# Turning q' two tiles at a time, and new places for the pieces of Wr

## The chip, the cores and the metric

The kernel runs on one core of a Trainium2 chip. The metric is the time of one execution on the device in microseconds; lower is better. Everything is 32-bit floating point outside; inside, each operand of a matmul is split into a high and a low part, so that three matmuls (high x high, high x low, low x high) stand for one exact product.

## The reference

`x` is 2048 x 576. Two branches are mixed by a gate for each row:

```python
g = sigmoid((x * gate_w).sum(-1, keepdims=True))
# A: linear attention, 32 heads of 18, phi(t) = where(t > 0, t + 1, exp(t)) + 1e-6
q, k, v = split(x @ wqkv); pq, pk = phi(q), phi(k)
kv  = einsum("bhsd,bhse->bhde", pk, v);  z = sum of pk over s
num = einsum("bhqd,bhde->bhqe", pq, kv); den = einsum("bhqd,bhd->bhq", pq, z) + 1e-6
a = (num / den).reshape(S, D) @ wo
# B: real part of a two-dimensional Fourier transform, with given matrices
y = dft_seq_re @ (x @ dft_hid_re.T) - dft_seq_im @ (x @ dft_hid_im.T)
return g * a + (1 - g) * y
```

## The kernel before, in words

TensorE works on tiles of 128 rows of `x` (16 tiles, `NT`) and half rows of 288 columns. The stages follow each other on TensorE:

- **k'** (`k_half`): k' = phi(x Wk) tile by tile. The first four tiles go together (L520), the other twelve one by one in the loop over `i`. Each tile is 2 halves of 14 matmuls. ScalarE and VectorE make phi (`feature`: two ScalarE operations and one VectorE operation for a half), split k' (`k_split`) and split the coming x tiles (`split_next`).
- **k'^T x** (L676): 20 steps; in step `step` four chunks of x are multiplied with the k' tiles. The chunks come by `xg_load` from SP's queue, are split by `xg_next` (tile `c`, raw `craw`), and stand in a ring of four. `kv_step` follows with Wv. In the same loop the sum over k' (`zacc`), Wq's load and split, and Wo's loads are placed.
- **q'** (`q_tile`): q' = phi(x Wq), 16 tiles of 28 matmuls; one more column pair of Wq gives the gate's logit, which ScalarE turns to exp(-logit), and VectorE to 1 + that and its reciprocal. kv and Wo are joined to one 576 x 576 matrix M (`build_kv`, `build_m`, `move_m`, `split_m`). `normalise` is a generator of four steps for a pair of tiles and divides q' by its denominators.
- **M stage**: `transposed(i)` turns tile i of q' with TensorE (four blocks of 128 columns, and a fifth for the 64 columns that are left, written twice side by side in `twice`), splits it to `qs`, and 2 x 14 matmuls with M follow; ScalarE scales with the gate, and POOL's queue stores `att`.
- **Hidden** (L945) and **sequence** (L1100), twice: the Fourier branch by Strassen-like products of seven: first x with Wr (`Hidden.run`), then with the matrix `cr`, then Wi and `ci`. `Matrix.load` brings the pieces of `cr` and `ci` (`craw` there), `make` adds and splits them; `row` tiles hold the branch so far.

For the last stages operands are prepared beside the earlier ones, in generators that are advanced by `go` at places written out by hand. `Left(k, ...)` loads a piece of x on POOL's queue, adds, splits and stores it (`xb`, `xm`): five steps. `right(w, ...)` gives three pieces of Wr or Wi (`wb`, stored to `wm`), of six steps: load, two additions, two additions, high, low and store, low and store (the third piece, 96 rows, has a low of 32 rows and one store). Each `next` puts its instructions at that point of the engines' order.

The order of ScalarE and VectorE is the order of the program from the k' stage on, that of SP's queue throughout, and that of TensorE from the first `Hidden.run` on; TensorE is ordered by a planner before that. POOL has its queue to itself and takes its DMAs in order. `begin_after` ties a POOL load to an earlier ScalarE instruction (`done[-1]`). PSUM has eight banks of which each `bank()` takes one. SBUF is one arena in which `at` places tiles by hand, so a piece can only be where the bytes are free: a load into bytes that a store still reads waits for it.

Of the kernel before, what the change touches and what calls it, by code (L numbers as in the profile page):

```python
# [8 lines left out]
F = mybir.dt.float32  # L9
R = mybir.dt.float32r  # L10
# [4 lines left out]
P = 128  # L15
# [116 lines left out]
def kernel(  # L132
# [108 lines left out]

    acc = [at(ACC_AT + i * D * 4, [P, D], F, "acc") for i in range(NT)]

# [337 lines left out]
    def xg_next(lo_of=lo_of):  # L581
        if xg_raw:
# [84 lines left out]
    for c in range(5):  # L667
        ps = [bank(), bank()]
        passes = FULL if c < KC else FULL[:2]
        for q in range(NCU):  # L670
# [21 lines left out]
            if step == 0:  # L692
                add(zacc, acc[0], acc[1])
            elif step < NT - 1:
                add(zacc, zacc, acc[step + 1])
            if step == NT + 1:
# [12 lines left out]
            for k, j, o in ((6, 2, SLOT_AT + 15104), (NP, 6, ACC_AT)):  # L709
# [15 lines left out]
    def q_tile(i):  # L725
        xs = split.pop(0)
        if i == 0:
            split_next()
        for h in range(2):
            ps = bank()[:, :QH[h]]  # L730
            run(ps, steps(xs, lambda j: wqt.row(h, j)))
            g = gate[:, i:i + 1]
# [3 lines left out]
        nc.vector.tensor_scalar(g, g, 1.0, None, op0=ALU.add)  # L736
        nc.vector.reciprocal(out=g, in_=g)
        load_next()
        if i:
            split_next()  # L740

    pz_ring = Ring(T_AT + 40960, D * 4, 4)

    def normalise(k):
# [10 lines left out]
        for i in range(2):  # L755
            a = acc[2 * k + i].rearrange("p (h d) -> p h d", d=DH)
            nc.vector.scalar_tensor_tensor(a, a, EPS,
                                           d[:, i].unsqueeze(2).to_broadcast([P, H, DH]),
                                           op0=ALU.add, op1=ALU.mult)
            twices.append(at(T_AT + 36864 + (2 * k + i) % 8 * 512, [P, 2, REST], F, "twice"))  # L760
            rest = acc[2 * k + i][:, KC * P:]
            nc.vector.tensor_copy(out=twices[-1],
                                  in_=rest.unsqueeze(1).to_broadcast([P, 2, REST]))
            yield

    twices = []
    norms = (part for k in range(NT // 2) for part in normalise(k))


    qs_ring = Ring(T_AT + 50176, XS, 2)  # L770

    def transposed(i):

        xs, _ = new_xs("qs", qs_ring)
        banks = [bank(), bank()]
        twice = twices.pop(0)
        for c in range(5):
            a = acc[i][:, c * P:(c + 1) * P] if c < KC else twice.rearrange("p a b -> p (a b)")
            nc.tensor.transpose(banks[c // KC][:, (c % KC) * P:(c % KC + 1) * P], a, ident)  # L779
        hi_of(xs[:, 0:4], banks[0])  # L780
        lo_of(xs[:, 5:9], banks[0], xs[:, 0:4])
        hi_of(xs[:, 4], banks[1][:, :P])
        lo_of(xs[:, 9], banks[1][:, :P], xs[:, 4])
        return xs

# [5 lines left out]
    mraw = at(T_AT + 23040, [P, KC, D], F, "mraw")  # L791
    mrest = at(T_AT + 32256, [P, D], F, "mraw")

    def build_kv():
# [40 lines left out]
    def split_m(h):  # L835
        hi_of(mhi[:, :KC, half(h)], mraw[:, :, half(h)])
        lo_of(mlo[:, :, half(h)], mraw[:, :, half(h)], mhi[:, :KC, half(h)])
        hi_of(mhi[:, KC, half(h)], mrest[:, half(h)])
        lo_of(mhi[64:, KC, half(h)], mrest[64:, half(h)], mhi[64:, KC, half(h)])

    def m_row(h, j):
        return mhi[:, j, half(h)] if j <= KC else mlo[:, j - 5, half(h)]

    store_rest()
    wr_forms, wr_pieces = right(wr, wr_rest, ((0, T_AT + 60416), (1, T_AT + 76544),
                                              (2, T_AT + 60416)))
    xs_ring.at[3] = T_AT + 105664
    load_next()
# [6 lines left out]
    q_tile(2)  # L855
    next(norms)
    q_tile(3)
    go(wr_pieces[0])
    next(norms)
    build_m((0, 1))  # L860
    for i in range(4, NT):
        q_tile(i)
        build_m({4: (2, 3), 5: (4,)}.get(i, ()))
        for g in range(2 * (i - 4), min(2 * (i - 3), NG)):
            move_m(g)
        for k, j, n in ((0, 4, 2), (0, 5, 1), (0, 6, 2), (1, 4, 1), (1, 7, 2), (1, 8, 1),
                        (1, 11, 2), (2, 9, 1), (2, 13, 2), (2, 14, 1)):
            if i == j:
                go(wr_pieces[k], n)
        if i in (5, 8, 11, 12, 13):  # L870
            go(norms)
        if i == NT - 3:
            nxt = transposed(0)
        if i in (9, 10):
            split_m(i - 9)

# [182 lines left out]
    def sequence(m, g, src, dst, last=None, between=None):  # L1059
        late, held, stores, rest_lows = [], [], [], []  # L1060
        for n in range(NP * NB):
            j, b = divmod(n, NB)
            if b == 0:
                ps = {k: bank()[:, :HALF] for k in PRODUCTS}
# [3 lines left out]
            c = m.ready.pop(0)  # L1068
            m.load(n + 3)
            while stores:  # L1070
                stores.pop(0)()
            if n == 2:
                tick()
            if m.raws:
                new = m.make()
# [7 lines left out]
            if n == 1:  # L1083
# [3 lines left out]
                del pending[-2:]  # L1087
            elif n == 2:
                while rest_lows:
                    rest_lows.pop()()  # L1090
            end = last is not None and j == NP - 1
# [60 lines left out]
    made = {}  # L1152
    plan = {
        2: [(0, 1)], 3: [(0, 1)], 4: [(0, 1)], 5: [(0, 1)], 6: [(0, 1)], 7: [(1, 1)], 8: [(1, 1)],
        9: [(1, 1)], 10: [(1, 1)], 11: [(1, 1)], 12: [(7, 1)], 13: [(7, 1)], 14: [(7, 1)],
        15: [(7, 2)],
    }
    for i in range(NT):
        qs = nxt
        if i + 1 < NT:  # L1160
            nxt = transposed(i + 1)
        for h in range(2):
            ps = bank()
            run(ps[:, :HALF], steps(qs, lambda j: m_row(h, j)))
            done.append(nc.scalar.activation(acc[i][:, half(h)], ps[:, :HALF], AF.Copy,  # L1165
                                             scale=gate[:, i:i + 1]))
        nc.gpsimd.dma_start(out=att[i], in_=acc[i])
# [5 lines left out]
        for k, j, o in ((0, 0, SLOT_AT), (1, 3, SLOT_AT + 7 * XF),  # L1173
                        (NP - 1, 8, T_AT + (NP - 2) * TPAIR)):
            if i == j:
                left = Left(k, o, done[-1])
                made[k] = left.make()
                if k < 2:
                    hidden.take_x(k, left.c)
        if i == 7:  # L1180
# [4 lines left out]
        for p, j in ((1, 8), (2, 11), (3, 15)):  # L1185
            if i == j:
                hidden.load_rest(p)
        if i == 11:
            hidden.load_pair(2)
        if i in (13, 15):  # L1190
            for k in (0, 2) if i == 13 else (4, 6):
                hidden.load_x(3, k)
    nc.vector.tensor_scalar(gate_n, gate, -1.0, 1.0, op0=ALU.mult, op1=ALU.add)
# [35 lines left out]

    paced.enter_context(tc.manual_schedule(engines={mybir.EngineType.PE}))  # L1230
    first.load_rest(4)
# [96 lines left out]
```

## Time and profile before

| | us |
|---|---|
| three runs | 726.32, 727.18, 729.66; median 727.18 |
| the profiled execution | 726.95, of which 725.2 are the span of its instructions |
| TensorE busy | 720.0 (5444 matmuls) |
| VectorE, ScalarE, POOL busy | 600.5, 335.7, 57.1 |

The span is the time from the first to the last instruction of the profiled execution. A busy time is the union of an engine's instructions. "PE" is TensorE's matmuls and "PEld" its weight loads, which overlap them; "DVE" is VectorE, "ACT" ScalarE, "POOL" GpSimd, "SP" the engine that only issues DMAs. In a group's row stand the line of the helper that recorded it, the engine, the operation, out<-in by the names of the program, the shape, the count, then the busy time, the mean of one in ns, and the idle time of the engine before them with what ended it. L173 is the high of every split (`hi_of`), L183 the low (`lo_of`), L193 an addition (`add`), L203 a matmul of `run`.

### The profile page before, as it was taken

What the parts mean: (1) busy time and instruction counts of PE and PEld (TensorE: products, weight loads), DVE (VectorE), ACT (ScalarE), POOL (GpSimd) and SP (SyncE); (2) the same over time, 40 slices, a digit from 0 to 9 for tenths busy, and PEclk for the clock granted to TensorE, in tenths of its full rate; (3) what the DMA queues carried; (4) which work ended last, traced back from release to release, by engine and by line L of the source; (5) the groups of instructions that cost most, each with busy time, mean ns of one, the idle gap of its engine ahead of it and who ended that gap; (6) DMA issues with size and microseconds to landing.
All of it is one profiled execution on the core that took longest, in us unless ns stands there. A gap on an engine that the chain in (4) does not pass through costs nothing.

```text
span 725.2 us, 13882 instructions
## 1 busy us (share of the span) xinstructions
PE 720.0 (99%) x5444; PEld 718.8 (99%) x5444; DVE 600.5 (83%) x995; ACT 335.7 (46%) x522; POOL 57.1 (8%) x98
## 2 busy tenths in 40 slices
PE   9999999999999999999999999999999999999998
PEld 9999999999999999999999999999999999999997
DVE  5789867589999948989999989767889988788884
ACT  5998346588644444453344334323535332232231
POOL 1011300051032110000000000000000000000000
PEclk9999999999999999999999999999999999999999
DMA  7376795676477999744475675889963543444440
GB/s 256 90 275 221 265 341 176 239 219 231 149 238 285 338 324 379 236 154 139 163 246 176 226 242 179 295 294 396 380 228 129 174 146 136 159 147 150 153 153 33
DMA packets 54372, 158.82 MB, mean 219 GB/s; under 512 B 6436, under 2 KB 11108, under 8 KB 53284
## 3 DMA queue, kind: packets, MB, share of 16 engines
q1 hardware_dynamic: 45060, 118.90, 47.9%
q0 software_dynamic: 8960, 38.65, 14.6%
q8 instruction: 43, 0.70, 0.4%
q10 hardware_dynamic: 288, 0.39, 0.1%
q14 instruction: 21, 0.17, 0.1%
HBM read 115.05 MB, written 41.39 MB: 216 GB/s over the span
## 4 chain that ended last, share of the span: by engine, by line
PE 93%; DMA 3%; DVE 2%; issue 1%; POOL 0%; ACT 0%; SPq 0%; DVEq 0%; ACTq 0%; POOLq 0%
PE bank L1100 48%; PE bank L203 23%; PE bank L945 14%; PE bank L676 3%; PE bank L520 2%; PE bank L779 1%; DMA craw<-in_xg_dram 1%; DMA wraw<-in_wv_dram 1%; DMA xm<-xb 1%; DVE ys L193 1%; PE bank L229 1%; POOL xb L389 0%; PE bank L658 0%; DVE c L183 0%; ACT xb L173 0%
## 5 line engine op out<-in xcount | busy, mean ns | idle before, releaser
L1100 PE MATMUL bank<-fh,c 128*128 128x288 f32 x1792 | 355.1, 294 | 0.3 <-DVE c L183 0.3
L1100 PEld LDWEIGHTS bank<-fh,c 128*128 128x128 f32 x1792 | 286.8, 188 | 0.5 <-DVE c L183 0.5
L1100 PE MATMUL bank<-fl,c 128*128 128x288 f32 x896 | 263.6, 294 | 0.0
L173 ACT ACTIVATE c<-craw 128x1792 fp32r<-128x1792 f32 (+1 forms) x84 | 121.5, 1449 | 187.5 <-DVE craw L193 169.2
L1100 PEld LDWEIGHTS bank<-fl,c 128*128 128x128 f32 x896 | 168.7, 188 | 0.0
L183 DVE TENSOR_TENSOR c<-craw,c 128x1792 fp32r<-128x1792 f32 (+4 forms) x86 | 142.0, 1654 | 6.2 <-ACT c L173 6.1
L193 DVE TENSOR_TENSOR craw<-craw 128x256 f32<-128x256 f32 (+1 forms) x192 | 98.3, 512 | 23.9 <-DMA craw<-in_ci_dram 11.7
L203 PE MATMUL bank<-wd,xs 128*128 128x288 f32 (+1 forms) x784 | 105.9, 296 | 0.0
L203 PEld LDWEIGHTS bank<-wd,xs 128*128 128x128 f32 x784 | 104.6, 188 | 0.1
L945 PE MATMUL bank<-wf,xf 128*128 128x288 f32 x588 | 91.1, 295 | 0.0
L945 PEld LDWEIGHTS bank<-wf,xf 128*128 128x128 f32 x588 | 83.5, 189 | 0.0
L203 PE MATMUL bank<-mw,qs 128*128 128x288 f32 x448 | 63.2, 297 | 0.0
L676 PE MATMUL bank<-pk,c 128*128 128x288 f32 x448 | 61.2, 296 | 0.1
L676 PEld LDWEIGHTS bank<-pk,c 128*128 128x128 f32 x448 | 59.9, 189 | 0.5 <-ACT c L173 0.4
L203 PEld LDWEIGHTS bank<-mw,qs 128*128 128x128 f32 x448 | 59.9, 188 | 0.2 <-DVE qs L183 0.2
L367 DVE SCALAR_TENSOR_TENSOR acc<-bank,e 128x288 f32<-128x288 f32 x64 | 28.1, 453 | 19.8 <-ACT e L366 19.1
L193 DVE TENSOR_TENSOR ys<-bank,ys 128x288 f32<-128x288 f32 x63 | 28.8, 457 | 15.1 <-PE bank L1100 12.0
L183 DVE TENSOR_TENSOR fl<-fl,fh 128x864 fp32r<-128x864 f32 (+1 forms) x32 | 34.6, 1093 | 6.6 <-ACT fh L173 5.3
L173 ACT ACTIVATE fh<-fl 128x864 fp32r<-128x864 f32 (+1 forms) x32 | 29.9, 951 | 16.6 <-DVE fl L193 15.0
L945 PE MATMUL bank<-wf,xr 96*128 96x288 f32 x112 | 33.3, 298 | 0.0
L1165 ACT ACTIVATE acc<-bank,gate 128x288 f32<-128x288 f32 x32 | 16.1, 502 | 35.0 <-PE bank L203 34.8
L193 DVE TENSOR_TENSOR ys<-ys,bank 128x288 f32<-128x288 f32 x47 | 21.2, 450 | 12.3 <-PE bank L1100 11.8
(107 smaller groups left out, 664.9 us busy)
## 6 DMA issues: line engine op xcount, KB each, us to landing
xf<-xm SPq DMA_DIRECT2D x42, 512.0 KB, 9.0
craw<-in_cr_dram SPq DMA_DIRECT2D x32, 512.0 KB, 3.9
craw<-in_ci_dram SPq DMA_DIRECT2D x32, 512.0 KB, 3.4
xraw<-in_xa_dram SPq DMA_DIRECT2D x28, 320.0 KB, 3.5
xm<-xb POOLq DMA_DIRECT2D x8, 1024.0 KB, 6.8
wf<-wm SPq DMA_DIRECT2D x14, 576.0 KB, 5.8
xr<-xr SPq DMA_DIRECT2D x14, 448.0 KB, 8.0
xm<-xb POOLq DMA_DIRECT2D x8, 768.0 KB, 6.4
```

The source lines that it names most:

```text
L173: return nc.scalar.activation(dst, src, AF.Copy, bias=bias)
L183: nc.vector.tensor_tensor(out=dst, in0=src, in1=hi, op=ALU.subtract)
L193: nc.vector.tensor_tensor(out=dst, in0=a, in1=b, op=op)
L203: nc.tensor.matmul(ps, a, b, start=(n == 0), stop=(n == len(pairs) - 1))
L229: nc.tensor.matmul(warm[:, :P], ones_f, ones_f, start=True, stop=True)
L367: nc.vector.scalar_tensor_tensor(dst, ps, 0.0, e, op0=ALU.max, op1=ALU.add)
L520: nc.tensor.matmul(ps[i][h], x[:, i * P:(i + 1) * P], wkt.row(h, j), start=(c == 0 and n == 0), stop=(c == KC and n == 1))
L676: nc.tensor.matmul(ps[h][:, :HALF], t[:, a, k], pk[s][:, b, half(h)], start=(s == 0 and n == 0), stop=(s == NT - 1 and n == len(passes) - 1))
L779: nc.tensor.transpose(banks[c // KC][:, (c % KC) * P:(c % KC + 1) * P], a, ident)
L945: nc.tensor.matmul(ps, a, b, start=(start and n == 0), stop=(n == len(ops) - 1), skip_group_check=True)
L1100: nc.tensor.matmul(ps[q], c[x][:, l, k], factors[p](y, f), start=(p == 0 and i == 0), stop=(p == NP - 1 and i == 2))
L1165: done.append(nc.scalar.activation(acc[i][:, half(h)], ps[:, :HALF], AF.Copy, scale=gate[:, i:i + 1]))
```

## The change

`transposed` takes a pair of tiles: eight transposes for the blocks of 128 columns, and one for the 2 x 64 columns that are left of both (`last`). Of that one, one half of the rows belongs to each tile; the high goes to one half of a block of `qs`, the low to the other half. `m_steps` lists the 14 matmuls of a half tile for this form; M's last rows are split whole (`mlast`). TensorE's written order starts ahead of the M stage. The gate's addition and reciprocal are made once for all tiles. q' goes through the tiles in the order 12 to 15, 0 to 11 (`TURNED`), so that the split x of tiles 12, 13 and 14 is kept from k' (`KEPT`). Wr's piece 1 moves from q' to the k' loop, piece 0 from q' to k'^T x, piece 2 stands wholly in q', and so does Left 7 (`seven`), which stood at the end of the M stage. `normalise` is advanced further in q'. The sum `zacc` goes through the tiles from the last. In the first `sequence` Wi's steps are taken in batches (`late`), and `m.load` stands ahead of the loads of the rows.

```diff
+KEPT = 3
+TURNED = [(i - KEPT - 1) % NT for i in range(NT)]
...
-    order += list(range(FT, NT)) + list(range(NT))
+    order += list(range(FT, NT)) + TURNED[KEPT:]
...
+    wr_forms, wr_pieces = right(wr, wr_rest, ((0, ACC_AT + 6144), (1, T_AT + (NP - 1) * TPAIR),
+                                              (2, T_AT + 76544)))
+    kept = []
     for i in range(FT, NT):
         xs = split.pop(0)
+        if i >= NT - KEPT - 1:
+            kept.append(xs)
...
-        if i < NT - 1:
+        if i in (4, 7, 8, 9, 10, 11):
+            go(wr_pieces[1])
+        if i < NT - FT:
             load_next()
...
-            if step in (1, 2):
-                split_next(lo_later)
...
+            if step in (13, 15, 16, 17, 18, 19):
+                go(wr_pieces[0])
...
     def q_tile(i):
-        xs = split.pop(0)
-        if i == 0:
-            split_next()
+        xs = kept.pop(0) if i < KEPT else split.pop(0)
...
-        nc.vector.tensor_scalar(g, g, 1.0, None, op0=ALU.add)
-        nc.vector.reciprocal(out=g, in_=g)
...
+    def transposed(k):
+        both = [at(qs_ring.next(), [P, 9, P], R, "qs") for _ in range(2)]
+        mains = [bank(), bank()]
+        last = bank()[:, :P]
+        for i in range(2):
+            for c in range(KC):
+                cs = slice(c * P, (c + 1) * P)
+                nc.tensor.transpose(mains[i][:, cs], acc[2 * k + i][:, cs], ident)
+        nc.tensor.transpose(last, lasts.pop(0).rearrange("p a b -> p (a b)"), ident)
+        for i, t in enumerate(both):
+            hi_of(t[:, 0:4], mains[i])
+            lo_of(t[:, 4:8], mains[i], t[:, 0:4])
+        for i, t in enumerate(both):
+            mine, other = ((slice(0, REST), slice(REST, P))[j] for j in (i, 1 - i))
+            hi_of(t[mine, 8], last[mine])
+            lo_of(t[other, 8], last[mine], t[mine, 8])
+        return both
...
+    def m_steps(qs, h):
+        for c in range(KC):
+            yield qs[:, c], mhi[:, c, half(h)]
+            yield qs[:, c], mlo[:, c, half(h)]
+            yield qs[:, 4 + c], mhi[:, c, half(h)]
+        yield qs[:, 8], mhi[:, KC, half(h)]
+        yield qs[:, 8], mlast[:, half(h)]
...
+    early = {4: [(norms, 2)], 5: [(norms, 1), (wr_pieces[2], 1)],
+             6: [(norms, 1)], 7: [(wr_pieces[2], 1)],
+             8: [(wr_pieces[2], 1)], 9: [(wr_pieces[2], 1), ("seven", 1)],
+             10: [("seven", 1)], 11: [(wr_pieces[2], 1)],
+             12: [(wr_pieces[2], 1), ("seven", 1), (norms, 1)], 14: [("seven", 1), (norms, 1)],
+             15: [("seven", 1), (norms, 1)]}
...
-        for k, j, n in ((0, 4, 2), (0, 5, 1), (0, 6, 2), (1, 4, 1), (1, 7, 2), (1, 8, 1),
-                        (1, 11, 2), (2, 9, 1), (2, 13, 2), (2, 14, 1)):
-            if i == j:
-                go(wr_pieces[k], n)
-        if i in (5, 8, 11, 12, 13):
-            go(norms)
...
-        if i in (9, 10):
-            split_m(i - 9)
+        if i in (10, 11):
+            split_m(i - 10)
...
+            m.load(n + 3)
             if b == 0:
...
             c = m.ready.pop(0)
-            m.load(n + 3)
...
+    nc.vector.tensor_scalar(gate, gate, 1.0, None, op0=ALU.add)
+    nc.vector.reciprocal(out=gate, in_=gate)
...
+    paced.enter_context(tc.manual_schedule(engines={mybir.EngineType.PE}))
     for i in range(NT):
-        qs = nxt
-        if i + 1 < NT:
-            nxt = transposed(i + 1)
+        qs, t = queue.pop(0), TURNED[i]
+        if i % 2 and i + 1 < NT:
+            queue += transposed(i // 2 + 1)
...
-        if i == 0:
-            go(wr_pieces[2], 2)
...
     def late(n):
-        k, part = divmod(n - 4, 7)
-        if 0 <= k < 3 and part != 1:
-            go(wi_pieces[k])
+        for k, parts in enumerate(((1, 5, 5, 5, 9, 9), (10, 13, 13, 13, 17, 17), (18, 21, 21, 21, 22, 22))):
+            go(wi_pieces[k], parts.count(n))
```

More of the change, by code (lines that the diff above doesn't have):

```diff
@@ L240 @@
     dens = Ring(small_at[0], 2 * H * 4, 2)
-    acc = [at(ACC_AT + i * D * 4, [P, D], F, "acc") for i in range(NT)]
+    acc_pairs = [at(ACC_AT + k * XD, [P, 2, D], F, "acc") for k in range(NT // 2)]
+    acc = [t[:, i] for t in acc_pairs for i in range(2)]
     raws, split = [], []
@@ L759, in normalise @@
                                            op0=ALU.add, op1=ALU.mult)
[L760 to L763, printed above, removed]
+            if i == 1:
+                lasts.append(at(last_ring.next(), [P, 2, REST], F, "last"))
+                nc.vector.tensor_copy(out=lasts[-1], in_=acc_pairs[k][:, :, KC * P:])
             yield
-    twices = []
+    lasts, last_ring = [], Ring(T_AT + 92672, 2 * REST * 4, 3)
     norms = (part for k in range(NT // 2) for part in normalise(k))
[L770 to L784, printed above, removed]
+    qs_ring = Ring(T_AT + 46592, 9 * P * 4, 3)
+    def transposed(k):
[15 more added lines that the diff above has]
+        return both
     kvb = at(C_AT, [GW, NG, 2, GW], R, "kvb")
@@ L855 @@
     q_tile(2)
-    next(norms)
+    go(norms, 1)
     q_tile(3)
-    go(wr_pieces[0])
-    next(norms)
+    go(norms, 2)
     build_m((0, 1))
+    early = {4: [(norms, 2)], 5: [(norms, 1), (wr_pieces[2], 1)],
[4 more added lines that the diff above has]
+             15: [("seven", 1), (norms, 1)]}
     for i in range(4, NT):
+        for part in early.get(i, ()) if i > 12 else ():
+            go(seven if part[0] == "seven" else part[0], part[1])
         q_tile(i)
         build_m({4: (2, 3), 5: (4,)}.get(i, ()))
+        if i == 6:
+            seven = Left(NP - 1, T_AT + (NP - 2) * TPAIR, done[-1]).make()
         for g in range(2 * (i - 4), min(2 * (i - 3), NG)):
             move_m(g)
-        for k, j, n in ((0, 4, 2), (0, 5, 1), (0, 6, 2), (1, 4, 1), (1, 7, 2), (1, 8, 1),
-                        (1, 11, 2), (2, 9, 1), (2, 13, 2), (2, 14, 1)):
-            if i == j:
-                go(wr_pieces[k], n)
-        if i in (5, 8, 11, 12, 13):
-            go(norms)
+        for part in early.get(i, ()) if i < 13 else ():
+            go(seven if part[0] == "seven" else part[0], part[1])
         if i == NT - 3:
-            nxt = transposed(0)
-        if i in (9, 10):
-            split_m(i - 9)
+            queue = transposed(0)
+        if i in (10, 11):
+            split_m(i - 10)
     factors, backlog = [], []
```

53 lines of the change are left out of this document (22 added, 31 removed).

## The prediction, on record before the result

> **What bounds the kernel now.** I read the busy times first, then the same times cut at the kernel's stages, then what the weight loads of TensorE waited for, and last the chain of waits. The first part of the page:
>
> ```profile
> PE 720.0 (99%) x5444; PEld 718.8 (99%) x5444; DVE 600.5 (83%) x995; ACT 335.7 (46%) x522; POOL 57.1 (8%) x98
> ```
>
> TensorE is busy for 720.0 of 725.2 us. So the time is a count of matmuls times their spacing, and another engine costs something only where it makes TensorE wait. The stages, as windows (k' after its first four tiles, k'^T x, q', the product with M):
>
> ```profile
> core 0: us, PE busy (x) PEld busy (x) DVE busy (x) ACT busy (x) POOL busy (x), PEclk, DMA share, GB/s
> 20.00:64.50 44.50, 44.50 (x337) 44.50 (x337) 37.07 (x69) 40.55 (x87) 5.20 (x8) 1.00 0.61 208
> 64.50:134.00 69.50, 69.37 (x531) 68.96 (x530) 52.83 (x88) 36.17 (x66) 9.16 (x14) 1.00 0.75 264
> 134.00:195.00 61.00, 61.00 (x462) 60.90 (x461) 51.99 (x121) 47.13 (x113) 14.54 (x24) 1.00 0.63 203
> 195.00:262.50 67.50, 67.49 (x521) 67.26 (x521) 59.81 (x119) 32.15 (x71) 15.65 (x26) 1.00 0.78 274
> ```
>
> TensorE is full in each, at a granted clock of 1.00. The others have room, but little: in k' ScalarE is busy 40.55 of 44.50 us and VectorE 37.07; in the M stage VectorE 59.81 of 67.50. The waits of the weight loads say what can be won back:
>
> ```profile
> PEld bank L1100 <- DVE c L183: 0.5, 1, 0.5
> PEld bank L676 <- ACT c L173: 0.4, 1, 0.4
> PEld bank L203 <- DVE qs L183: 0.2, 1, 0.2
> PEld bank L676 <- DVE c L183: 0.2, 1, 0.2
> ```
>
> That is 1.3 us in the whole kernel: 0.5 in the big product, 0.6 in k'^T x, 0.2 in the M stage. From the chain of waits (start, length, what) I take the spacings:
>
> ```profile
> 19.86 44.59 PE bank L203 x336
> ...
> 99.72 7.72 DMA craw<-in_xg_dram
> ...
> 125.11 4.24 PE bank L676 x32
> ...
> 212.27 3.71 PE bank L203 x28
> 215.98 0.55 PE bank L779 x5
> ```
>
> A tile is 28 matmuls in 3.71 us, 0.1327 us each. The five transposes of a tile (L779) take 0.55 us, 0.11 each.
>
> **The change, part by part.** The profiled execution took 726.95 us: the span of 725.2 and 1.75 around it. It lies 0.23 below the median of the three runs (727.18). I make the sum against 726.95.
>
> *One transpose for both rests.* Before, 16 tiles have 5 transposes, 80; after, 8 pairs have 9, 72. The matmuls stay at 14 a half tile (the old list had 4x3 + 2, `m_steps` has 4x3 + 2). Eight transposes less at 0.55/5 = 0.11 give -0.88 us, and since TensorE has no idle time for them to hide in, all of it counts. The groups of these transposes show another number:
>
> ```profile
> L779 PE MATMUL bank<-ident,acc 128*128 128x128 f32 x64 | 9.6, 272 | 0.0
> L779 PE MATMUL bank<-ident,twice 128*128 128x128 f32 x16 | 4.4, 273 | 0.0
> ```
>
> One lasts 272 ns, but they overlap; the spacing in the chain is what the end sees. [...]
>
> *What VectorE and ScalarE lose and get.* The groups, mean ns behind the comma:
>
> ```profile
> L183 DVE TENSOR_TENSOR wb<-wb 128x1152 fp32r<-128x1152 f32 x4 | 5.4, 1352 | 0.0
> L183 DVE TENSOR_TENSOR wb<-wb 128x864 fp32r<-128x864 f32 x4 | 4.2, 1052 | 0.0
> L183 DVE TENSOR_TENSOR wb<-wb 32x2016 fp32r<-32x2016 f32 x2 | 4.5, 2250 | 0.5 <-ACT wb L173 0.5
> L193 DVE TENSOR_TENSOR wb<-wb 128x288 f32<-128x288 f32 x16 | 7.1, 456 | 0.3
> L173 ACT ACTIVATE wb<-wb 128x2016 fp32r<-128x2016 f32 x4 | 7.5, 1884 | 1.0 <-DVE wb L193 1.0
> L183 DVE TENSOR_TENSOR mw<-mraw,mw 128x1152 fp32r<-128x1152 f32 x2 | 2.7, 1359 | 0.2 <-ACT mw L173 0.2
> L367 DVE SCALAR_TENSOR_TENSOR acc<-bank,e 128x288 f32<-128x288 f32 x64 | 28.1, 453 | 19.8 <-ACT e L366 19.1 <-PE bank L203 0.4
> L737 DVE RECIPROCAL gate<-gate 128x1 f32<-128x1 f32 x16 | 2.6, 164 | 0.5
> L736 DVE TENSOR_SCALAR gate<-gate 128x1 f32<-128x1 f32 x16 | 2.3, 144 | 0.0
> L762 DVE COPY twice<-acc 128x128 f32<-128x128 f32 x16 | 3.8, 235 | 0.6
> L183 DVE TENSOR_TENSOR qs<-bank,qs 128x512 fp32r<-128x512 f32 x16 | 10.9, 684 | 1.3 <-ACT qs L173 1.2
> ```
>
> A full piece of Wr is 4 additions of 0.456, two lows of 1.352 and 1.052 and one high of 1.884: 4.23 us of VectorE, 1.88 of ScalarE. Piece 1 leaves q' for k', piece 0 leaves q' for k'^T x. Besides, 32 small gate operations (16 x (0.164 + 0.144) = 4.9 us) become two, and 16 copies become 8 (-1.9 us).
>
> *k' (piece 1).* VectorE would go to 37.07 + 4.23 = 41.3 and ScalarE to 40.55 + 1.88 = 42.4 of 44.5 us: full, but not over. What TensorE waits for here is the next tile's split x, two to three tiles ahead. Line L203 runs 12 tiles in 44.59 us, 3.716 each, from 19.86, so tiles 11, 12, 13 and 14 begin at 45.87, 49.59, 53.30 and 57.02. Their splits in the timeline of VectorE:
>
> ```profile
> 43.26 0.82 DVE L183 TENSOR_TENSOR xs<-xraw,xs 128x640 fp32r<-128x640 f32 x1
> ...
> 46.06 0.82 DVE L183 TENSOR_TENSOR xs<-xraw,xs 128x640 fp32r<-128x640 f32 x1
> ...
> 48.96 0.46 DVE L367 SCALAR_TENSOR_TENSOR acc<-bank,e 128x288 f32<-128x288 f32 x1 [0.26 <-ACT e L366]
> 49.60 0.83 DVE L183 TENSOR_TENSOR xs<-xraw,xs 128x640 fp32r<-128x640 f32 x1 [0.17 <-PE bank L203]
> 52.20 0.46 DVE L367 SCALAR_TENSOR_TENSOR acc<-bank,e 128x288 f32<-128x288 f32 x1 [1.78 <-ACT e L366]
> ...
> 54.18 0.82 DVE L183 TENSOR_TENSOR xs<-xraw,xs 128x640 fp32r<-128x640 f32 x1 [0.17 <-ACT xs L173]
> ```
>
> They end 1.79, 2.71, 2.87 and 2.02 us ahead of use. Piece 1 puts four additions (1.82) ahead of tiles 11 and 12: 0.03 late, then in time. Tile 13 also has the low of 1.35 ahead, less idle time of 0.26 + 0.17: 2.74 against 2.87. Tile 14 has 1.82 + 1.35 + 1.05 = 4.22, less 0.26 + 0.17 + 1.78 + 0.17: 1.84 against 2.02. ScalarE's 1.88 falls on its own 3.95 us of idle time. So it fits, by a tenth or two: +0.1 us, between 0 and +0.5.
>
> *k'^T x (piece 0).* VectorE has 16.7 us idle, and two x splits leave it, so its 4.23 us are hidden. The price would be on the DMA queues: the piece's load is issued at step 13, beside the last loads of `craw`. The chain's `craw` load took 7.72 us, when stores of Left 5 were under way, and TensorE waited for it (the 0.4 + 0.2 above). The DMA list has the usual one, and the timeline the last split, of 0.42 us:
>
> ```profile
> craw<-in_xg_dram SPq DMA_DIRECT2D x20, 256.0 KB, 3.8
> ```
> ```profile
> 124.39 0.42 DVE L183 TENSOR_TENSOR c<-craw,c 128x256 fp32r<-128x256 f32 x1 [2.60 <-ACT c L173]
> ```
>
> That split is ready at 124.81; the 16 matmuls that use it are the second half of the 32 from 125.11, from 127.23. Cover: 2.4 us. If the new load slows one `craw` as far as 7.72 (+3.9), TensorE waits 1.5. If moved work shifts the old collision away, 0.6 is won. Nearest is the old row, with the same loads in the same order: 0, between -0.6 and +1.5. The stores of piece 0 come at steps 18 and 19, behind all `craw` loads, and the first acc tile they read (tile 2) is written again at the end of the third q' tile, 11 us (3 x 3.71) into that stage, where a slow transfer like the chain's takes 7.72. 0.
>
> *q' (piece 2, Left 7, more normalisation).* 8.5 us of Wr, 4.9 of gates and one split leave; what comes is Left 7, the whole of piece 2 and three more steps of normalisation, so VectorE stays near 52 of 61 us. The dense place is behind tile 11: the low of 2.25 and half of M's split (1.36 and a smaller one, 1.8 together), with a tile's own features and x split (2 x 0.45 + 0.82): 5.8 us in a tile of 3.7, 2.1 behind. The split of tile 14 is done in order two tiles ahead, with some 1.4 to 1.8 to spare: +0.3, between 0 (before, 2.40 of piece 1 passed there) and +0.7.
>
> *M stage.* VectorE loses the copies, piece 2's low and Left 7. The 0.2 for `qs` should go: -0.2. The gate's two operations stand ahead of ScalarE's first scaled copy; behind that wait only the copies of two banks of eight. Transposes now stand in written order ahead of the odd tile, so the pair's split has 28 matmuls (3.7 us) of cover and needs 0.98 of transposes, a high and a low of 0.684 each for the first tile: hidden. The normalised pair is one pair ahead. 0.
>
> *Wi's batches, load order in the big product.* The pieces' steps leave the steps in which results are moved out; the one wait, 0.5, comes late in the first product, where piece 2's low lies. Additions and high now come together: I take half, -0.25, between -0.5 and +0.3. The `craw` load ahead of two row loads removes a possible wait only: 0.
>
> Sum: 726.95 - 0.88 + 0.1 + 0 + 0.3 - 0.2 - 0.25 = 726.0 us.
>
> **The rivals.**
> *Slower: the stores on the way of the SP queue.* Piece 1's load and stores stand on POOL's queue ahead of the DMAs of Left 3 to 5. SP's `wqt` loads wait for Left 5's stores, and behind them stand the `craw` loads; the first of them has no cover left (0.6 already waited), so from the first microsecond by which Left 5's stores come later, TensorE pays one for one. If two of these loads come 3.9 later, the first without cover and a second with the 2.4 found above, it costs 3.9 + 1.5 = 5.4: 731.4. Against it: piece 1's stores are issued at tiles 10 and 11, near 50 us, 50 us ahead of the 99.72 row. [...] Chance 0.09.
>
> *VectorE's batches stop the big product.* Three additions-and-high batches and three of lows; if each costs the 0.5 that the one wait cost, 6 x 0.5 = 3.0 less the 0.5 gone: 728.8. For it: VectorE's one wait is there. Chance 0.06.
>
> *The transposes save nothing.* Pairing needs three banks and both tiles at once; if the first tile of each later pair waits as `qs` did (0.2), 7 x 0.2 takes 1.4 back: 727.4. Chance 0.10.
>
> *Transposes cost their whole duration.* 8 x 0.272 = 2.18 for 0.88: 724.7. Against it: five in 0.55. [...] Chance 0.03.
>
> **How the numbers follow.** The forecast has 0.72. 0.5%, about what a measurement of this kernel can tell from no change, is 3.6 us: the borders are 723.5 and 730.8. Faster would need all 1.3 us of waits and more than twice the transposes: 0.02. Slower is the first rival: 0.09. The rest, 0.89, is the same. Low end: 726.0 - 0.25 - 0.6 - 0.3 - 0.1 = 724.7, less 0.5 by which a run may lie lower: 724.2. High end: 726.0 + 0.4 (k') + 0.4 (q') + 1.5 (k'^T x) + 0.25 = 728.55, with the median's 0.23: 728.8, which holds the second rival too.
>
> **What would show it.** Transposes x72, nine in about 0.98 us; no wait of L203 for `qs`; in k' waits of weight loads for `xs` of at most some tenths; the window of the M stage about 0.9 to 1.1 us shorter. It is wrong if TensorE waits for more than 2 us in any stage after the first matmul, if `craw` loads land later than 108 us, or if the spacing of 0.1327 moves.

## The result and the profile after

The changed kernel takes 733.22 us (median of six runs, 731.74 to 735.29) where the kernel before takes 728.17 beside it: ratio 1.0068, 95% interval 1.0048 to 1.0087. The forecast was 726.0, with a range to 728.8: it is wrong by 7 us and in its sign. The sum started from 726.95; as a change, -0.95 us was forecast and +5.05 measured. The profiled executions have spans of 730.7 and 725.2 us. Cut at the first matmul of each stage:

| stage, us | before | after | difference |
|---|---|---|---|
| start, first four tiles of k' | 19.70 | 19.97 | +0.27 |
| k', 12 tiles | 44.59 | 44.59 | 0 |
| k'^T x | 64.91 | 67.06 | +2.15 |
| q' and M | 133.17 | 136.72 | +3.55 |
| first Hidden | 52.02 | 51.98 | -0.04 |
| first sequence | 177.84 | 177.17 | -0.67 |
| second Hidden and sequence, to the last matmul | 229.12 | 229.12 | 0 |

Two stages lose. The table shows one execution of each kernel; the granted clock differs among the six of the changed kernel, 1.000 in the one of 731.74 us and 0.995 in those of 734.29 and 735.29. The page's first part, and the waits of the weight loads, which name two stops (columns: who waited, for whom; us in total, times, longest):

```profile
PE 721.2 (99%) x5436; PEld 719.2 (98%) x5436; DVE 594.3 (81%) x954; ACT 332.8 (46%) x519; POOL 57.2 (8%) x98
```
```profile
PEld bank L686 <- DVE c L185: 2.6, 2, 2.1
PEld bank L205 <- ACT xs L175: 2.4, 1, 2.4
PEld bank L231 <- POOL ones_f L227: 1.2, 1, 1.2
PEld bank L205 <- DVE qs L185: 0.4, 1, 0.4
PEld bank L205 <- DVE xs L185: 0.3, 1, 0.3
```

The row `ones_f` is the start, the same in both kernels. Eight matmul records are gone (5436 for 5444): the transposes. Lines have moved: L185 is the low, L175 the high, L195 an addition, L205 `run`, L686 k'^T x.

**The stop in k'^T x**, at 102.9 us. VectorE's timeline of the changed kernel (start, length; in brackets the idle time before and what ended it):

```profile
97.69 0.75 DVE L195 TENSOR_TENSOR zacc<-zacc,acc 128x576 f32<-128x576 f32 x1
102.80 1.56 DVE L195 TENSOR_TENSOR xb<-xb 128x256 f32<-128x256 f32 x4 [4.36 <-DMA xb<-in_xq_dram]
104.28 0.68 DVE L185 TENSOR_TENSOR c<-craw,c 128x512 fp32r<-128x512 f32 x1
```

VectorE stands 4.36 us at the additions of Left 8 (the x rest, made from step 6 on), and the low of `c` that TensorE needs is queued behind them. What they wait for is Left 8's four loads. POOL's timeline before (L389 those loads, L408 the stores of Left 5 and 6, L383 the loads of the other Lefts) and after (L392, L411, L386):

```profile
81.38 1.47 POOL L383 DMA_DIRECT2D xb<-in_xq_dram  x2 [5.96 <-DMA xm<-xb]
85.31 2.17 POOL L389 DMA_DIRECT2D xb<-in_xq_dram  x3 [2.46 <-DVE xb L183]
89.03 0.72 POOL L389 DMA_DIRECT2D xb<-in_xq_dram  x1 [1.55 <-issue]
89.75 1.12 POOL L408 DMA_DIRECT2D xm<-xb  x2
```
```profile
82.96 1.46 POOL L386 DMA_DIRECT2D xb<-in_xq_dram  x2 [7.27 <-ACT c L175]
85.58 0.58 POOL L411 DMA_DIRECT2D xm<-xb  x1 [1.16 <-DVE xb L185]
86.95 0.56 POOL L411 DMA_DIRECT2D xm<-xb  x1 [0.79 <-DVE c L185]
88.27 0.72 POOL L392 DMA_DIRECT2D xb<-in_xq_dram  x1 [0.76 <-DVE zacc L195]
89.74 0.74 POOL L392 DMA_DIRECT2D xb<-in_xq_dram  x1 [0.75 <-issue]
93.29 0.74 POOL L392 DMA_DIRECT2D xb<-in_xq_dram  x1 [2.81 <-issue]
95.77 0.72 POOL L392 DMA_DIRECT2D xb<-in_xq_dram  x1 [1.74 <-issue]
```

Before, the four loads go ahead of the two stores and are issued by 89.03. After, the stores go first, the first load waits for an addition to `zacc`, and the last is issued at 95.77. The chain of waits has it land 7.01 us later:

```profile
95.77 7.01 DMA xb<-in_xq_dram
```

**The stop in q'**, at 143.7 us. The chain of waits, then SP's timeline (L422 the six stores of Left 8, L259 the x tiles), then POOL's (L457 the stores of Wr's piece 0):

```profile
134.82 10.57 DMA xraw<-in_xa_dram
145.39 0.02 issue
145.41 0.74 ACT xs L175
146.16 0.02 issue
146.18 0.84 DVE xs L185
```
```profile
128.57 6.15 SPq L422 DMA_DIRECT2D xr<-xb  x6
134.82 9.55 SPq L259 DMA_DIRECT2D xraw<-in_xa_dram  x4
```
```profile
132.68 0.77 POOL L457 DMA_DIRECT2D wm<-wb  x1 [17.90 <-DVE wb L185]
134.24 0.76 POOL L457 DMA_DIRECT2D wm<-wb  x1 [0.79 <-DVE wb L185]
```

The x of the fourth q' tile is the first that is not kept from k'. Its load stands behind six stores, is issued 0.6 us after the second of piece 0's two, and takes 10.57 us. Around it, by windows:

```profile
core 0: us, PE busy (x) PEld busy (x) DVE busy (x) ACT busy (x) POOL busy (x), PEclk, DMA share, GB/s
134.80:143.70 8.90, 8.90 (x71) 8.90 (x70) 3.52 (x8) 3.73 (x10) 0.20 (x1) 1.00 1.01 360
143.70:147.50 3.80, 1.56 (x10) 1.08 (x9) 1.21 (x3) 1.39 (x4) 0.00 (x0) 1.00 0.84 309
147.50:150.90 3.40, 3.40 (x18) 3.40 (x17) 2.75 (x9) 2.57 (x9) 0.00 (x0) 0.58 0.00 0
```

While the load is on its way the DMA engines are full (share 1.01). And the stop costs more than itself: behind it the granted clock falls to a mean of 0.58 in the third window; only 18 matmuls run there, where 3.40 us hold 25.6 at a spacing of 0.1327. The clock's own record has 0.5 for 3.41 us, so 1.7 us are lost. Waits of 2.4 + 0.3 and 1.7 of clock, less the 0.75 that the stage saves (below), make 3.65 us, and the table has 3.55; in k'^T x the waits grew by 2.6 - 0.6 = 2.0, and the stage by 2.15.

### The profile page after: what moved, and what is told of

Same layout as the page of the kernel before. It is cut to its first block, busy times and chain, and to the rows that moved or that the text cites. A ratio compares the mean times of both kernels' runs of the same rounds, so it can differ in the third digit from the quotient of the medians.

```text
span 730.7 us, 13799 instructions
## 1 busy us (share of the span) xinstructions
PE 721.2 (99%) x5436; PEld 719.2 (98%) x5436; DVE 594.3 (81%) x954; ACT 332.8 (46%) x519; POOL 57.2 (8%) x98
## 4 chain that ended last, share of the span: by engine, by line
PE 87%; DVE 6%; DMA 3%; issue 2%; ACT 1%; POOL 0%; DVEq 0%; ACTq 0%; POOLq 0%
PE bank L1118 48%; PE bank L205 17%; PE bank L964 14%; PE bank L686 4%; PE bank L523 2%; DMA xraw<-in_xa_dram 1%; DVE qs L185 1%; DVE acc L763 1%; DMA craw<-in_xg_dram 1%; DMA xb<-in_xq_dram 1%; DVE pz L755 1%; DVE den L756 1%; DVE xb L185 1%; ACT xb L175 1%; PE bank L231 1%
## 5 line engine op out<-in xcount | busy, mean ns | idle before, releaser
L175 ACT ACTIVATE c<-craw 128x1792 fp32r<-128x1792 f32 (+1 forms) x84 | 121.4, 1448 | 187.9 <-DVE craw L195 163.3
L185 DVE TENSOR_TENSOR c<-craw,c 128x1792 fp32r<-128x1792 f32 (+4 forms) x86 | 142.0, 1653 | 4.2 <-ACT c L175 4.1
L195 DVE TENSOR_TENSOR craw<-craw 128x256 f32<-128x256 f32 (+1 forms) x192 | 98.0, 512 | 22.6 <-DMA craw<-in_ci_dram 14.3
L205 PE MATMUL bank<-wd,xs 128*128 128x288 f32 (+1 forms) x784 | 107.9, 298 | 2.2 <-ACT xs L175 2.2
L205 PEld LDWEIGHTS bank<-wd,xs 128*128 128x128 f32 x784 | 106.2, 191 | 2.7 <-ACT xs L175 2.4
L686 PE MATMUL bank<-pk,c 128*128 128x288 f32 x448 | 61.2, 296 | 2.2 <-DVE c L185 2.2
L686 PEld LDWEIGHTS bank<-pk,c 128*128 128x128 f32 x448 | 59.8, 188 | 2.8 <-DVE c L185 2.6
L205 PE MATMUL bank<-mw,qs 128*128 128x288 f32 x448 | 61.8, 296 | 0.1
L205 PEld LDWEIGHTS bank<-mw,qs 128*128 128x128 f32 x448 | 59.8, 188 | 0.5 <-DVE qs L185 0.4
L195 DVE TENSOR_TENSOR ys<-bank,ys 128x288 f32<-128x288 f32 x63 | 28.8, 457 | 16.1 <-PE bank L1118 12.8
L185 DVE TENSOR_TENSOR fl<-fl,fh 128x864 fp32r<-128x864 f32 (+1 forms) x32 | 34.5, 1093 | 6.5 <-ACT fh L175 5.3
L175 ACT ACTIVATE fh<-fl 128x864 fp32r<-128x864 f32 (+1 forms) x32 | 29.8, 950 | 16.8 <-DVE fl L195 16.8
L195 DVE TENSOR_TENSOR fl<-bank,y 128x288 f32<-128x288 f32 x48 | 21.6, 451 | 15.7 <-PE bank L964 15.7
L195 DVE TENSOR_TENSOR ys<-ys,bank 128x288 f32<-128x288 f32 x47 | 21.2, 450 | 11.7 <-PE bank L1118 11.2
```

The source lines that it names most:

```text
L175: return nc.scalar.activation(dst, src, AF.Copy, bias=bias)
L185: nc.vector.tensor_tensor(out=dst, in0=src, in1=hi, op=ALU.subtract)
L195: nc.vector.tensor_tensor(out=dst, in0=a, in1=b, op=op)
L205: nc.tensor.matmul(ps, a, b, start=(n == 0), stop=(n == len(pairs) - 1))
L686: nc.tensor.matmul(ps[h][:, :HALF], t[:, a, k], pk[s][:, b, half(h)], start=(s == 0 and n == 0), stop=(s == NT - 1 and n == len(passes) - 1))
```

## The experiments

Each kernel is the changed one but for its diff. "k'^T x to M" is the time from the first matmul of k'^T x to the first of the first Hidden: 198.08 us before, 203.78 after. Ratios are to the kernel before, with 95% intervals.

**The stop in q'.** First the load of the x tile ahead of the six stores:

```diff
-    store_rest()
     xs_ring.at[3], xs_ring.n = T_AT + 34560, KEPT
     load_next()
+    store_rest()
```

> The load of the fourth q' tile stands ahead of the six stores of Left 8 on SP's queue instead of behind them; nothing else moves. Theory A (that load lost its time in a queue of stores, its own queue's and piece 0's): the 2.4 us wait for xs goes, and with it the half clock after it (3.4 us at 0.5, 1.7 us): about 4.1 us less than the changed kernel's 733.2, 729.1. Rival (the transfer engines are full until piece 0's last store lands at 145.2, so where the load stands is of no use): the wait stays over 1.5 us, 732 to 733. The wait of 2.1 us in k'^T x stays by both.

Measured: 729.64 us, ratio 1.0033 (1.0021 to 1.0046), k'^T x to M 199.77. No wait for `xs` is left, and in the profile the clock stays at 1.00. Then piece 0 back in q', where the kernel before has it:

```diff
-    wr_forms, wr_pieces = right(wr, wr_rest, ((0, ACC_AT + 6144), (1, T_AT + (NP - 1) * TPAIR),
+    wr_forms, wr_pieces = right(wr, wr_rest, ((0, T_AT + 60416), (1, T_AT + (NP - 1) * TPAIR),
...
-            if step in (13, 15, 16, 17, 18, 19):
-                go(wr_pieces[0])
...
     q_tile(3)
+    go(wr_pieces[0])
...
         build_m({4: (2, 3), 5: (4,)}.get(i, ()))
+        go(wr_pieces[0], {4: 2, 5: 1, 6: 2}.get(i, 0))
```

> Piece 0 of Wr is back in q' on its old places (load behind tile 3, its steps behind tiles 4, 5 and 6), in the bytes it had before; the rest of the change stays, the order of SP's queue too. Theory A1 (piece 0's two stores made the load of the fourth q' tile slow): the load takes some 6 us instead of 10.6, the 2.4 us wait and the half clock go, 729.1, less or more up to 1 us because VectorE has 4.2 us more in q'. Theory A2 (the six stores of Left 8 ahead of it do it alone, the change only lost the cover): the wait stays over 1.5 us, 732 to 734. The wait of 2.1 us in k'^T x stays by both.

Measured: 728.53 us, ratio 1.0013 (1.0003 to 1.0024), k'^T x to M 199.18. Here the six stores still stand ahead of the load, and nothing waits. So it takes both: the load's place behind six stores, and piece 0's two stores beside it. By the ratios the two repairs give 2.5 and 4.0 us, and in the profiles k'^T x to M is 4.0 and 4.6 us shorter. Both kernels keep the stop in k'^T x; the waits of the weight loads of the second, from 85 us to the end of the M stage:

```profile
PEld bank L686 <- DVE c L185: 2.4, 2, 1.9
PEld bank L205 <- DVE qs L185: 0.4, 1, 0.4
```

**The stop in k'^T x: four wrong or blunt attempts.** Piece 1 back in q' (in other bytes than before, a line of its diff that is left out here):

```diff
-        if i in (4, 7, 8, 9, 10, 11):
-            go(wr_pieces[1])
...
+        go(wr_pieces[1], {4: 1, 7: 2, 8: 1, 11: 2}.get(i, 0))
```

> Piece 1 of Wr is back in q' (load behind tile 4, steps behind tiles 7, 8 and 11) in bytes that are free there; the order of POOL's queue in k'^T x stays that of the changed kernel, Left 8's loads behind Left 5's stores. Theory B2 (piece 1's transfers in k'): the 2.1 us wait in k'^T x goes, 731.1, plus up to 1 us because VectorE has 4.2 us more in q'. Theory B1 (the place of Left 8's loads): it stays over 1 us, 732 to 734. The wait for xs in q' stays by both.

Measured: 734.57, ratio 1.0110 (1.0086 to 1.0134). In k'^T x the waits fall from 2.6 to 1.6 us. But q' keeps its stop (2.0 and 0.3 for `xs`; the mean clock of the profiled execution is 0.998, as in the changed kernel) and has two new waits near 195 us, 1.5 for `acc` and 0.8 for `xs`. So the total says nothing of the stop in k'^T x, and there piece 1 is a part of the cause, not the whole. Next, Left 8 begun one step earlier, which puts its loads ahead of the stores on POOL:

```diff
-            for k, j, o in ((6, 2, SLOT_AT + 15104), (NP, 6, ACC_AT + 22528)):
+            for k, j, o in ((6, 2, SLOT_AT + 15104), (NP, 5, ACC_AT + 22528)):
```

> Left 8's loads are asked for one step earlier (step 5), which puts them ahead of Left 5's stores on POOL's queue, where they stood in the kernel before. Theory B1 (their place behind these stores made them land at 102.8 instead of 92.1, and VectorE stood on Left 8's first addition with the low of c behind it): the 2.1 us wait in k'^T x goes, 731.1. Theory B2 (the transfers of piece 1 in k' delay everything that POOL's queue does after): the wait stays over 1 us, 732 to 733.5. The wait for xs in q' stays by both.

Measured: 741.25, ratio 1.0189 (1.0144 to 1.0233). Both expectations missed, by 7.8 us and more. VectorE's timeline says why, and it became the key to the rest:

```profile
95.50 0.76 DVE L195 TENSOR_TENSOR zacc<-zacc,acc 128x576 f32<-128x576 f32 x1 [8.38 <-DMA xb<-in_xq_dram]
```

An addition of a tile of `acc` to `zacc` waits 8.38 us for Left 8's load, though the two share no byte (the addition is that of tile 8, see below). TensorE waits 6.7 and later 2.4, and behind the first the clock is 0.50 (98.4 to 104.0 us). Next, Left 8's additions moved behind the lows of two later steps:

```diff
-            if q < NCU - 1:
+            if q < NCU - 1 and step not in (9, 10):
                 left_part()
```

> Only the place of Left 8's parts in program order is changed (none is issued after the big products of steps 9 and 10), everything else is the changed kernel. Theory V (the 2.1 us stop of TensorE at 102.9 us is VectorE's first-in-first-out queue: the low half of the next piece of k'^T x stands behind Left 8's additions, which wait for a load that lands at 102.8): the low halves are no longer behind that wait, the stage k'^T x falls from 67.06 to 65 to 66 us (a wait for a late xg load of up to 1 us may stay), and the whole falls by 1.2 to 2.1 us against the changed kernel: 731.1 to 732.0 where that was 733.2, ratio to before about 1.004 to 1.006, with the second stop (q') still there. Theory T (the transfers themselves are late for TensorE, whatever VectorE's order): the stop stays at 1.5 to 2.7 us and the time stays 732.5 to 734.

Measured: 731.81, ratio 1.0066 (1.0044 to 1.0087). That is in theory V's range, but not by its mechanism: k'^T x to M takes 203.16 us, only 0.6 less than in the changed kernel. The stop at 102.9 is gone, but one of 2.3 us stands at 116.6 instead: there the low of `c` is queued behind Left 8's own lows and one of Wq's, all late by now.

```profile
114.69 0.76 DVE L185 TENSOR_TENSOR wd<-wraw,wd 128x580 fp32r<-128x580 f32 x1 [1.98 <-ACT wd L175]
115.37 0.75 DVE L195 TENSOR_TENSOR zacc<-zacc,acc 128x576 f32<-128x576 f32 x1
116.03 2.21 DVE L185 TENSOR_TENSOR xb<-xb,xb 128x1024 fp32r<-128x1024 f32 x2
118.16 0.68 DVE L185 TENSOR_TENSOR c<-craw,c 128x512 fp32r<-128x512 f32 x1
```

VectorE's order was therefore only where the lateness shows, not its source. The same edit with each repair of q' agrees:

> The two repairs together: the load of the last q' tile ahead of the six stores on SyncE's queue (which alone gave 729.64, ratio 1.0033) and Left 8's parts later. Theory V with the first one: 727.5 to 728.4, ratio 0.9995 to 1.001, k'^T x 65 to 66 us and q' with M 132.4 as with the first repair alone. Theory T: 729 to 730 as with the first repair alone. If the prediction's sum was right but for the two stops, the profile's span is 724.3 to 725.3.

> Wr's piece 0 back in q' (alone 728.53, ratio 1.0013) and Left 8's parts later. Theory V: 726.4 to 727.6, ratio 0.998 to 1.000, k'^T x 64.9 to 65.9 us: no stop of over 1 us anywhere, and the profile's span 724.0 to 725.0, as the prediction's sum had it. Theory T: 728 to 729.

Measured: 730.13, ratio 1.0038 (1.0020 to 1.0055), and 730.96, 1.0048 (1.0031 to 1.0066): no better than the repairs alone (the second is worse than its own 1.0013), against the theory. And the two edits on piece 1 and step 5 together:

> Wr's piece 1 back in q' (so that its two stores no longer stand in GpSimd's queue at 55.2 and 56.4 us, ahead of Left 4's stores) and Left 8 begun one step earlier, so that its four loads stand ahead of Left 5's stores on GpSimd's queue, as in the kernel before. Theory P (both together make Left 8's loads late: piece 1 shifts GpSimd's queue by some 4 us at 66 us, and the order puts the stores ahead): loads issued by 90 us, landed by 93, k'^T x 64.9 to 65.4 us (before 64.91). Theory W (another cause, such as the step at which Left 8's additions stand in VectorE's order, or the xg loads): k'^T x 66 us or more. q' has its own stops here from piece 1 (as with piece 1 alone moved back, 734.6), so the stage decides and not the total; total about 733 to 735 by P, 735 to 740 by W.

Measured: 742.33 in one run, k'^T x 74.7. Loads issued by 89.7, nearly as in the kernel before, and yet the stage is 9.8 us longer than there; only step 5 alone makes it longer (77.4). That fell too.

**One cause: pairs.** The 8.38 us row says that a tile of `acc` which Left 8 does not overwrite counts as overwritten. The change has, besides what was told of it:

```diff
-    acc = [at(ACC_AT + i * D * 4, [P, D], F, "acc") for i in range(NT)]
+    acc_pairs = [at(ACC_AT + k * XD, [P, 2, D], F, "acc") for k in range(NT // 2)]
+    acc = [t[:, i] for t in acc_pairs for i in range(2)]
```

A tile has 576 x 4 = 2304 bytes. Left 8's new place begins at 22528 = 9.78 tiles, in tile 9. The new sum goes downwards and takes tile 9 in step 5, tile 8 in step 6. With single tiles Left 8 may load after step 5, as before; with pairs it must wait for tile 8, which shares tile 9's pair: the `zacc` in the brackets of 88.27. By then Left 5's stores are ahead. Undone:

```diff
-    acc_pairs = [at(ACC_AT + k * XD, [P, 2, D], F, "acc") for k in range(NT // 2)]
-    acc = [t[:, i] for t in acc_pairs for i in range(2)]
+    acc = [at(ACC_AT + i * D * 4, [P, D], F, "acc") for i in range(NT)]
...
-            if i == 1:
+            if i == 0:
                 lasts.append(at(last_ring.next(), [P, 2, REST], F, "last"))
-                nc.vector.tensor_copy(out=lasts[-1], in_=acc_pairs[k][:, :, KC * P:])
+            nc.vector.tensor_copy(out=lasts[-1][:, i], in_=acc[2 * k + i][:, KC * P:])
```

> Only this is undone: the 16 tiles of acc are 16 tiles again and not 8 pairs (the rests of two tiles are copied into `last` by two small copies in place of one). Theory A (the pairs make Left 8's loads late: its place begins in tile 9 of acc, which shares a pair with tile 8, so its loads must wait for the sum of tile 8, one step later, and the stores of Left 5 go ahead of them on GpSimd's queue): the four loads are ahead of the stores again, the last lands by 96 us, VectorE's wait ahead of Left 8's additions is under 1 us, k'^T x takes 64.7 to 65.6 us in place of 67.06; the second stop, in q', stays (unless its load comes to lie elsewhere), so 731 to 732 in place of 733.2, ratio about 1.004 to 1.006. Theory P (Wr's piece 1 in k' makes GpSimd's queue late whatever the order, as the later Left parts only moved the stop to 116.6 us): k'^T x 66.4 us or more, a stop of 1.5 to 2.5 us somewhere between 91 and 118 us, 732.5 to 734.

> Single tiles of acc, and the load of the last q' tile ahead of the six stores on SyncE's queue (alone 729.64, ratio 1.0033). Theory A: no stop of over 0.7 us in k'^T x or q', k'^T x to M 197.2 to 198.0 us together (before 198.08), and with the 0.67 us of the big product the whole is 726.3 to 727.5 where before is 727.5, ratio 0.9985 to 1.000: the prediction's sum. Theory P: 729 to 730.5.

> Single tiles of acc, and Wr's piece 0 back in q' (alone 728.53, ratio 1.0013). Theory A: as the kernel above, k'^T x to M 197.0 to 197.8 us, 726.0 to 727.3, ratio 0.998 to 1.000. Theory P: 728.5 to 730.

Measured: 731.38, ratio 1.0037 (1.0023 to 1.0051); with the load first 728.73, 1.0007 (0.9997 to 1.0016); with piece 0 back 728.60, 1.0010 (0.9999 to 1.0021). In the first, Left 8's loads are ahead of the stores, the last lands at 93.4, and the stop of 2.1 us is gone. That is what theory A said, and so is the time; but the stage k'^T x takes 66.52 us, or 65.9 without five matmuls of q' that stand ahead of its end here, where A said at most 65.6 and P at least 66.4. Two waits are new or longer, 1.3 at 108 us for a `craw` load that lands at 108.6 (before: 0.4, landing 107.4) and 1.0 for `qs`, where the two copies of `last` now stand ahead of the split in VectorE's order. In the second, k'^T x to M is 199.08, not the 197.2 to 198.0 expected, and the time lies between the two theories. In the third it is 200.60, not 197.0 to 197.8, and the time lies in theory P's range: over piece 0 alone (1.0013) single tiles gain nothing that can be told apart. So theory A has a cause and not the whole size. Next, the pairs kept, the load of the fourth q' tile ahead of the six stores as in the first experiment, and the sum moved (the load's diff is left out):

```diff
-            elif step < NT - 1:
+            elif step < NT - 1 and step != 6:
                 add(zacc, zacc, acc[NT - 2 - step])
+                if step == 5:
+                    add(zacc, zacc, acc[NT - 3 - step])
```

> The changed kernel with its pairs of acc kept, the load of the last q' tile ahead of the six stores (alone 729.64, ratio 1.0033), and tile 8 of acc summed one step earlier, together with tile 9, so that the pair under Left 8's place is free at step 5. Theory A (the pair delays Left 8's loads): they stand ahead of Left 5's stores again, the stop at 102.9 us is gone, k'^T x to M takes 198.1 to 199.0 us (as with single tiles, 199.08, less the some 0.5 us that two small copies in place of one cost there in the M stage), 727.3 to 728.5 where before is 728, ratio 0.9985 to 1.0005. Rival (the pairs don't matter; with single tiles it was another order of VectorE's work that helped): the stop of 1.9 us at 103 us stays, 729.3 to 730, ratio 1.002 to 1.004.

Measured: 728.33 us (twelve runs, 726.56 to 730.47) beside 728.04, ratio 0.9999 (0.9985 to 1.0012), where the load alone had 1.0033. One addition, 0.75 us of VectorE at another place, decides the order on POOL, and the wait for `qs` is 0.3. This is the best version of the change, and it is level with the kernel before. In its profile less is gained: k'^T x to M is 199.23, a little over the 198.1 to 199.0 expected, for 199.77 with the load alone. (The profile with the load alone shows an execution of 728.20 us, where the median is 729.64.) Its waits of the weight loads from 80 to 115 us, and POOL's rows:

```profile
PEld bank L686 <- DVE c L185: 1.7, 3, 1.1
PEld bank L686 <- ACT c L175: 0.6, 1, 0.6
```
```profile
85.86 1.46 POOL L386 DMA_DIRECT2D xb<-in_xq_dram  x2 [10.05 <-DMA xm<-xb]
87.31 0.73 POOL L392 DMA_DIRECT2D xb<-in_xq_dram  x1
90.14 2.15 POOL L392 DMA_DIRECT2D xb<-in_xq_dram  x3 [2.11 <-issue]
```

**The other cause: piece 1 on POOL's queue.** The loads at 85.86 were at 81.38 before. Is that piece 1, whose two stores stand on POOL's queue at 55.15 and 56.38 in the changed kernel, ahead of Left 3's (the expectation calls them Left 4's)? The kernel just shown, with piece 1 in q' as above:

> As the kernel with tile 8 summed early and the q' load first, and besides Wr's piece 1 back in q' (there it has stops of its own, as with piece 1 alone moved back; they are not the question). Theory P' (the waits of 1.1, 0.5 and 0.6 us that stayed in k'^T x come from piece 1's two stores at 55 and 56 us, which shift Left 4's stores and with them all of GpSimd's queue by some 4 us): Left 4's stores issue at 57 and 60 us as before, Left 8's loads land by 93 us, and TensorE's waits between 85 and 112 us are 0.3 to 0.8 us together (before: 0.5), where they were 1.9. Rival R (they come from something else in the change): still 1.5 us or more. The whole about 730 to 733 by both, because of q'.

Measured: one run, 731.11, slower by q' as expected; but in k'^T x POOL is as before, 1 us later as the whole stage is, and the waits from 80 to 115 us are 0.8 together (before: 0.6):

```profile
82.38 1.47 POOL L386 DMA_DIRECT2D xb<-in_xq_dram  x2 [6.69 <-DMA xm<-xb]
86.37 2.17 POOL L392 DMA_DIRECT2D xb<-in_xq_dram  x3 [2.52 <-DVE xb L185]
90.19 0.72 POOL L392 DMA_DIRECT2D xb<-in_xq_dram  x1 [1.65 <-issue]
```
```profile
PEld bank L684 <- ACT c L175: 0.6, 1, 0.6
PEld bank L684 <- DVE c L185: 0.2, 1, 0.2
```

So piece 1 in k' is free in k', where the prediction costed it, and is paid in k'^T x: 2.3 - 0.8 = 1.5 us by these two profiles. The way there, in the kernel with the sum moved (in brackets the kernel before): piece 1's stores put Left 3's at 60.33 and 61.90 (56.72 and 59.84); Left 5's loads, which take the bytes of Left 3, start at 70.11 (65.50), and Left 6's, which take those of Left 4, at 85.86 (81.38). The two causes side by side, by the waits of the weight loads from 80 to 115 us, one profile each:

| Left 8's loads | piece 1 in k' | piece 1 in q' |
|---|---|---|
| behind Left 5's stores | 2.6; with q's load repaired 3.0 | 1.6 |
| ahead of them | 2.3 | 0.8 |

The order is worth 0.7 to 0.8 us of these waits, piece 1's place 1.0 to 1.5. The order's gain in the ratios, 2.5 us, is larger than its waits; what the rest is was not isolated.

## Why the prediction was wrong, point by point

- *Transposes, M stage.* The transposes are right: a pair with its nine takes 8.41 us from one round to the next, where two tiles with their ten took 2 x 4.26, which makes -0.9 in eight pairs for the forecast -0.88. With the q' stop gone and nothing else changed, q' and M take 132.42 us for 133.17: -0.75, where the terms -0.88, -0.2 and +0.3 gave -0.78. That the sum fits is luck, as two terms failed against each other: no wait stands for the +0.3 of q', and the wait for `qs`, which was to go (-0.2), is 0.4 for 0.2. Duration times eight (the fourth rival) would be -2.2. The trace's -0.9 stands against it. The third rival falls by the -0.75; a wait for `qs` is there once.
- *k'.* Right: 44.59 in both, forecast +0.1.
- *Wi's batches.* Sign right, size too small: the 0.5 wait is gone, and the stage takes -0.67 for -0.25, outside the -0.5 allowed; no wait explains the last 0.1. The second rival falls.
- *k'^T x: this step failed.* It said 0, at most +1.5, "with the same loads in the same order". They were not: Left 8's loads changed places with Left 5's stores. The step followed `craw` on SP and never asked POOL what Left 8's loads wait for: a new place, in a tile of double size, under a sum in a new order. The stage measured +2.15. By the waits, 0.7 to 0.8 of that are the order, and 1.0 to 1.5 piece 1, which the prediction costed in k' alone (+0.1). It also took the stores beside the `craw` load of 7.72 us (99.72 to 107.44) for Left 5's; those had landed by 97.03, and Left 6's, issued at 95.60 and 96.95, were under way.
- *Piece 0's stores, "0": this failed too.* The step asked who reads what the stores still hold (`acc`), not who shares the DMA engines with them (share 1.01 while that load is on its way). The cover that it needed to name is that of the fourth q' tile's load, which the change puts behind six stores. Measured: 2.4 + 0.3 of waits.
- *The clock.* No term. A wait was priced at its length; behind this one, in the profiled execution, the clock was halved for 3.41 us, 1.7 more.
- *The first rival* had the right kind (stores in the way of loads, 731.4 at 0.09) with another load. Its part with piece 1 on POOL's queue was set aside because 50 us lay between; yet up to 1.5 us came through, from one load that waits for the bytes of a store to the next.

The sign that the prediction named for being wrong, a wait of over 2 us in a stage, came twice.

## What to carry to other kernels

When operands move, list for each DMA that is left in place what it now waits for and what stands ahead of it on its queue: a merged tile or a reversed loop changes that without a line of the DMA's own being touched (here the last of Left 8's loads went from 89.03 to 95.77 us). A tile that is merged for one reader's sake is merged for every writer's wait as well (here an addition to `zacc` waited 8.38 us for a load of other bytes). And where an in-order engine stops, look for the latest load behind it before changing that engine's order: here moving the waiting work only moved the stop, from 102.9 to 116.6 us.

## What the hardware showed that was not expected

The granted clock was halved behind some stops and not behind others. In the changed kernel it is 0.50 for 3.41 us from 148.04 us on, behind the waits of 2.4 and 0.3 for `xs`, and stays at 1.00 behind the 2.1 us at 102.9. In the kernel with step 5 its mean is 0.74 from 92 to 96 us, 0.50 from 96 to 104 and 0.98 from 104 to 108: from within the 6.7 us wait on, an estimated 10.2 us at half clock by these means. In these traces length alone does not decide: with both repairs of VectorE's order and SP's load, a wait of 2.1 us was followed by a half clock and one of 2.3 was not. The windows behind the two:

```profile
95.20:98.50 3.30, 3.30 (x15) 3.30 (x15) 3.30 (x6) 1.08 (x3) 1.13 (x2) 0.50 0.44 168
123.00:126.40 3.40, 3.40 (x25) 3.40 (x26) 2.59 (x6) 0.78 (x2) 0.00 (x0) 1.00 0.26 92
```

What decides between them was not shown: no run varied a stop for that alone.

POOL's queue has pauses that no semaphore ends ("issue", 2.81 us at 93.29). The load then issued came 0.3 us after an earlier transfer of the same queue had landed (92.97), and so it was at 95.77 (95.43), and in the kernel before at 89.03 (88.71). In the changed kernel such pauses make 5.3 of the 7.5 us between the first and the last of Left 8's loads. What they wait for was not shown, as no run varied it.
